# Second token pair's first block sums during h times M, casts by kind, and products that wait for their own part of a weight pair

## The chip, the cores and the metric

The kernel runs on one core of a Trainium2 chip. The metric is the device time of one launch in microseconds, the median of three runs.

## The reference

An attention with mixing of heads before and after the softmax, then two chained feed-forward layers, all in float32:

```python
scores = scale * np.matmul(q, k.transpose(0, 1, 3, 2))          # 4 x 12 heads, 448 x 64
scores = np.einsum('bhij,hg->bgij', scores, w_pre)
attn = softmax(scores)                                          # over the last axis
attn = np.einsum('bhij,hg->bgij', attn, w_post)
x = np.matmul(attn, v)                                          # -> 1792 tokens x 768
h = (x @ w1) * (x @ w2)                                         # 1792 x 1024
x = (h @ w3) @ w_out                                            # 1792 x 768
h = x @ w_in                                                    # 1792 x 2048
out = np.square(np.maximum(h, 0)) @ w_out2                      # 1792 x 768
```

## The kernel before

Every float32 operand of a product is split into two float16 halves, high and low, and a product is three matmuls (high x high, high x low, low x high). A cast of an operand is thus two instructions: ScalarE writes the high half (`nc.scalar.activation` with AF.Copy), VectorE the low half (`scalar_tensor_tensor`, the scaled operand minus its high half).

The stages, with their place in the profiled execution: attention to about 425 us; the two hidden products and their product h to 655; M = w3 x w_out, which takes the place of two products, to 725 (`m_tile`, matmuls L1520); h x M to 836 (matmuls L1243, evicted by ScalarE L1710); x times w_in to 1036 (`multiply_in`, L1847); and the last product with w_out to the end (`multiply`, L2099).

The last two stages use a seven-product scheme for 2 x 2 blocks. Of a weight pair q = 0..7 there are the blocks A11, A12, A22 and the sums S1 to S4; of a token pair t = 0, 1 the blocks B11, B21, B22 and the sums T1 to T4. S3 = a11 - a21, S1 = a21 + a22, S2 = S1 - a11, S4 = a12 - S2; T1 = b12 - b11, T3 = b22 - b12, T2 = b22 - T1, T4 = b21 - T2. GpSimd makes the sums, ScalarE and VectorE the casts. Each of the seven products of (q, t) is 9 matmuls of 448 columns. TensorE takes them in the order A11 of the n-th pair, S1 of the one before, S3, A12, S2, S4 of the one before, A22; the pairs (q, t) come as (0,0), (1,0), (2,0), (1,1), (2,1), (0,1), (3,0) and so on.

The work beside the products is written as Python generators (streams), each a chain of steps with an engine and a planned cost. `tick(us)` is called behind products in the code and advances the planned time by that much; the planner then takes steps whose engine is free by plan. What it takes is put into the engine's queue there, and each engine runs its queue in that order. `finish(stream)` takes all that is left of a stream at once.

The streams that matter here are:

- `form_in` (L1061): per weight pair q it loads two blocks (tiles ib), makes the four sums on GpSimd (L1073) and casts them on ScalarE (L1124) and VectorE (L1125), into tile w for q = 0 and wq from q = 1. For q below 3 the sums lie in two tiles it: ta with sums[0] = S1 and sums[1] = S2, tb with S3 and S4, where the positions in wq are A11, A12, A22, then ta, then tb. A product asks `need_in(q)`, which takes steps until all of the pair is cast.
- `x2_steps` (L1654): for a token pair, per block column c of three, the casts B (ScalarE L1434, VectorE L1430) and the sums T on GpSimd (L1658). It begins for t = 1 when the last eviction of h x M is issued. B11 of t = 1 is cast before, in a stream `first_of`.
- `keep_m` (L1499): in the M stage, copies of the two product banks by ScalarE, and as a stream the reductions of their largest values on VectorE (L1261). In the same stage VectorE decodes weights that come in packed, with three instructions each (L776, L779, L783), then ScalarE and GpSimd split them (L991, L994) into the operand w of the M products. `m_tile` ticks 0.163 per product bank after each of the three matmuls of a bank.
- `mixed_tokens` (L1966): in the w_out stage, for each of 14 token tiles, four sums on GpSimd (L1969) and seven casts on ScalarE (L1991) and VectorE (L1992). The products' evictions are ScalarE's L2113 and VectorE's L2115; those of the w_in stage are ScalarE's L1882 and L1892 and VectorE's L1884.

Of the kernel before, what the change touches and what calls it, by code (L numbers as in the profile page):

```python
# [34 lines left out]
def talking_heads_attention_moe_moe2(  # L35
# [1025 lines left out]
    def form_in():  # L1061

        for g in range(NF2 // IG):
            box = {}

            def sides(q):
                box["b"] = [flat(w_tile(1, "ib")) for _ in range(2)]
                flush("kept")
                for z in range(2):
                    nc.sync.dma_start(box["b"][z], kept_in[2 * q + z])  # L1070

            def mix(o, a, b, op=ALU.subtract):
                nc.gpsimd.tensor_tensor(o, a, b, op=op)  # L1073

            for q in range(g * IG // 2, (g + 1) * IG // 2):
                while ("in", 2 * q + 1) not in wsp:
# [4 lines left out]
                if q < 3:
                    ta, tb = (flat(w_tile(1, "it")) for _ in range(2))
                    sums = [ta[:, :OH], ta[:, OH:], tb[:, :OH], tb[:, OH:]]
                else:
                    while x_of[1] in streams:
                        yield REST, 0.5, lambda: finish(x_of[1])
                    sums = [stage()[:, :OH] for _ in range(4)]
                a11, a12, a21, a22 = x0[:, :OH], x0[:, OH:], x1[:, :OH], x1[:, OH:]
                for o, l, r, op in (
                    (sums[0], a21, a22, ALU.add), (sums[1], sums[0], a11, ALU.subtract),  # L1090
                    (sums[2], a11, a21, ALU.subtract), (sums[3], a12, sums[1], ALU.subtract),
                ):
# [4 lines left out]
                if q:
                    while not started or (q > 2 and q - 2 not in over):
                        yield REST, 0.5, lambda: None
                    w = fin_pool[0].tile([P, 2, 7, OH], F16, tag="wq", name="wq", bufs=2)  # L1100
                    ks = [w[:, :, k] for k in range(7)]

                    def where(k, n):
                        return [w[:, z, k : k + n].rearrange("p k o -> p (k o)") for z in range(2)]

                else:
                    ws = [w_tile(0).rearrange("p z (k o) -> p z k o", k=2) for _ in range(4)]
                    ks = [ws[k][:, :, z] for k, z in ((0, 0), (0, 1), (1, 0), (2, 0), (2, 1), (3, 0), (3, 1))]

                    def where(k, n):  # L1110
                        i, y = ((0, 0), (0, 1), (1, 0), (2, 0), (2, 1), (3, 0), (3, 1))[k]
                        return [ws[i][:, z, y : y + n].rearrange("p k o -> p (k o)") for z in range(2)]

                srcs = [(x0, 0, 2), (x1[:, OH:], 2, 1)]
                if q < 3:
                    srcs += [(ta, 3, 2), (tb, 5, 2)]
# [2 lines left out]
                parts = [(x, k, where(k, n)) for x, k, n in srcs]
                for x, k, (h, l) in parts:  # L1120
                    n = x.shape[-1] // OH
                    if k == 3:
# [524 lines left out]
    def xop(t, z, k, c):  # L1647
# [3 lines left out]
            return xs_[z][:, 7, c]  # L1651
        return xbig[0][:, z, k - 1, c]

    def x2_steps(t, ts):  # L1654
        box = {}

        def mix(o, a, b):
            nc.gpsimd.tensor_tensor(o, a, b, op=ALU.subtract)  # L1658

        def mixes(c):  # L1660
            b11, b12, b21, b22 = ts[c], ts[NDC + c], ts[c + 3], ts[NDC + c + 3]
            box[c] = {B11: b11, B21: b21, B22: b22, T1: b11, T2: b22, T3: b12, T4: b21}
            t1, t2, t3, t4 = (box[c][k] for k in (T1, T2, T3, T4))
            return [
                (POOL, 1.25, lambda: mix(t1, b12, b11)), (POOL, 1.25, lambda: mix(t3, b22, b12)),
                (POOL, 1.25, lambda: mix(t2, b22, t1)), (POOL, 1.25, lambda: mix(t4, b21, t2)),
            ]
# [8 lines left out]
        sums = [mixes(c) for c in range(3)]  # L1676
        for c in range(3):
            yield from casts(c, (B21, B22) if t else (B11, B21, B22))
            if t == 0:
                yield from sums[c]  # L1680
                yield after(POOL)
                yield from casts(c, (T3, T2, T4, T1))
            elif c:
                yield from sums[c - 1]
        if t:
            yield from sums[2]
            for k in (T3, T2, T4, T1):
                for c in range(3):
                    yield from casts(c, (k,))

    have_x, first_of = [set(), set()], []

    def casts_of(t, c, ks):
        yield from halves_steps(
            [([xop(t, z, k, c) for z in range(2)], x, x_scale[0][0]) for k, x in ks]
        )
        for k, _ in ks:
            have_x[t].add((k, c))
# [594 lines left out]
```

## Time and profile before

| | us |
|---|---|
| median of 3 runs | 1234.51 (1233.56 to 1236.69) |
| the profiled execution | 1236.24 |
| its span, first to last instruction | 1234.5 |
| TensorE busy | 1213.4 |
| VectorE busy | 948.6 |
| ScalarE busy | 804.5 |
| GpSimd busy | 581.6 |

The profile is that of one execution; its time lies a little above the median. TensorE is PE in the profile's rows, its weight loads PEld, VectorE is DVE, ScalarE ACT, GpSimd POOL. A row "x<-a,b" writes x from a and b. A releaser, as in "[3.17 <-DVE wq L1125]", is the instruction that ended an engine's idle time of that length.

### The profile page before, as it was taken

What the parts mean: (1) busy time and instruction counts of PE and PEld (TensorE: products, weight loads), DVE (VectorE), ACT (ScalarE), POOL (GpSimd) and SP (SyncE); (2) the same over time, 40 slices, a digit from 0 to 9 for tenths busy, and PEclk for the clock granted to TensorE, in tenths of its full rate; (3) what the DMA queues carried; (4) which work ended last, traced back from release to release, by engine and by line L of the source; (5) the groups of instructions that cost most, each with busy time, mean ns of one, the idle gap of its engine ahead of it and who ended that gap; (6) DMA issues with size and microseconds to landing.
All of it is one profiled execution on the core that took longest, in us unless ns stands there. A gap on an engine that the chain in (4) does not pass through costs nothing.

```text
span 1234.5 us, 26238 instructions
## 1 busy us (share of the span) xinstructions
PE 1213.4 (98%) x9904; PEld 749.2 (61%) x9904; DVE 948.6 (77%) x1690; ACT 804.5 (65%) x1620; POOL 581.6 (47%) x569
## 2 busy tenths in 40 slices
PE   7999999999999999999999999998999999999998
PEld 3666776677667655555558975554455555666665
DVE  6888899788889957766665875787578774999783
ACT  6788888888888735655554454567778785765430
POOL 3898788889878600110011211526124423667340
PEclk9999999999999999999999999999999999999999
DMA  6456555655645934755524547263478659565562
GB/s 186 123 156 166 141 146 134 169 128 155 171 114 164 260 98 120 159 143 163 133 94 145 171 146 243 76 207 103 143 269 289 237 169 320 180 189 181 171 201 77
DMA packets 139843, 205.02 MB, mean 166 GB/s; under 512 B 33764, under 2 KB 114788, under 8 KB 139716
## 3 DMA queue, kind: packets, MB, share of 16 engines
q1 hardware_dynamic: 136020, 200.01, 54.7%
q10 hardware_dynamic: 3136, 2.40, 0.8%
q8 instruction: 78, 1.28, 0.5%
q0 software_dynamic: 560, 0.93, 0.4%
q14 instruction: 49, 0.40, 0.1%
HBM read 114.60 MB, written 50.16 MB: 133 GB/s over the span
## 4 chain that ended last, share of the span: by engine, by line
PE 80%; DVE 9%; DMA 5%; ACT 2%; issue 1%; POOL 1%; SPq 0%; ACTq 0%; DVEq 0%; POOLq 0%
PE mm L1243 20%; PE mm L2099 15%; PE mm L1847 13%; PE p L284 10%; PE o L380 9%; PE s L241 5%; PE a L494 5%; DVE x L1430 2%; DMA Bt<-S 2%; PE p L1243 2%; DVE xa L776 1%; DVE xa L779 1%; DVE xa L783 1%; DMA raw<-in_moe_w_dram 1%; DVE wq L1125 1%
## 5 line engine op out<-in xcount | busy, mean ns | idle before, releaser
L1243 PE MATMUL mm<-x,w 128*128 128x448 f16 x1044 | 197.7, 352 | 0.0
L1847 PE MATMUL mm<-x,wq 128*128 128x448 f16 x882 | 172.7, 356 | 5.3 <-DVE wq L1125 3.7
L1243 PEld LDWEIGHTS <-w 128*128 128x128 f16 x1152 | 112.2, 98 | 104.3
L284 PE MATMUL p<-Bt,wpre_k 120*120 120x448 f32 x360 | 159.5, 561 | 4.9 <-DMA Bt<-S 4.2
L2099 PEld LDWEIGHTS <-ao 128*128 128x128 f16 x1176 | 115.0, 98 | 77.1 <-issue 1.2
L380 PEld LDWEIGHTS <-EH 120*112 120x112 f16 (+1 forms) x1440 | 124.9, 130 | 44.6 <-issue 37.1
L1847 PEld LDWEIGHTS <-wq 128*128 128x128 f16 x882 | 86.4, 99 | 87.4 <-DVE wq L1125 4.5
L353 POOL TENSOR_SCALAR EH<-E,st 120x448 f16<-120x448 f32 (+1 forms) x152 | 113.1, 752 | 49.1 <-DVE st L336 37.0
L402 DVE TENSOR_TENSOR ATl<-o,ATh 112x480 f16<-112x480 f32 x180 | 116.0, 645 | 22.3 <-ACT ATh L396 21.6
L306 ACT ACTIVATE E<-p,st 120x448 f32<-120x448 f32 x180 | 116.0, 645 | 22.9 <-DVE st L298 14.2
L396 ACT CAST ATh<-o 112x480 f16<-112x480 f32 x180 | 101.2, 562 | 44.3 <-PE o L380 39.4
L380 PE MATMUL o<-wph,EH 120*112 120x120 f16 x720 | 124.6, 219 | 1.0 <-DVE ATl L402 1.0
L380 PE MATMUL o<-wph,EL 120*112 120x120 f16 x720 | 122.6, 216 | 0.0
L380 PE MATMUL o<-wpl,EH 120*112 120x120 f16 x720 | 122.6, 216 | 0.0
L365 POOL TENSOR_TENSOR EL<-F,EH 120x448 f16<-120x448 f32 (+1 forms) x90 | 104.1, 1157 | 32.8 <-issue 19.9
L298 DVE TENSOR_REDUCE st<-p 120x1 f32<-120x448 f32 x180 | 110.1, 612 | 3.1 <-PE p L284 2.8
L1243 PE MATMUL mm<-h,M 128*128 128x448 f16 x576 | 110.2, 353 | 0.0
L2099 PE MATMUL mm<-x,ao 128*128 128x384 f16 x588 | 96.6, 326 | 1.0 <-ACT st L2113 1.0
L2099 PE MATMUL mm<-ow,ao 128*128 128x384 f16 x588 | 96.0, 326 | 0.0
L380 PEld LDWEIGHTS <-EL 120*112 120x112 f16 x720 | 93.9, 130 | 0.0
L367 DVE SCALAR_TENSOR_TENSOR EL<-E,st,EH 120x448 f16<-120x448 f32 (+1 forms) x90 | 83.6, 929 | 10.9 <-POOL EH L353 10.5
L1243 PEld LDWEIGHTS <-M 128*128 128x128 f16 x576 | 55.9, 98 | 52.0 <-DVE M L1430 0.8
(264 smaller groups left out, 2532.9 us busy)
## 6 DMA issues: line engine op xcount, KB each, us to landing
Bt<-S SPq DMA_DIRECT2D x176, 210.0 KB
raw<-in_moe_w_out_dram SPq DMA_DIRECT2D x24, 768.0 KB
g<-ev SPq DMA_DIRECT2D x64, 224.0 KB
gt<-g SPq DMA_DIRECT2D x56, 256.0 KB
raw<-in_moe_w_in_dram SPq DMA_DIRECT2D x16, 768.0 KB
raw<-in_moe_w_dram SPq DMA_DIRECT2D x14, 768.0 KB
raw<-in_moe_w_dram SPq DMA_DIRECT2D x16, 512.0 KB
kept_out<-xa SPq DMA_DIRECT2D x16, 384.0 KB
```

Source lines behind the costliest of these rows:

```text
L284: nc.tensor.matmul(pt[: n * H, :S], wpre_k.rearrange("p t g -> p (t g)")[: n * H, : n * H], Bt.pop(u)[: n * H], start=True, stop=True,)
L298: nc.vector.tensor_reduce(nsum[u][:n, 0, j : j + 1], Pp[u][:n, :S], axis=AX.X, op=ALU.max, negate=True)
L306: nc.scalar.activation(e[:n], Pp.pop(u)[:n, :S].rearrange("p (a b) -> p a b", a=EG), AF.Exp, bias=t[:n, 0, j : j + 1], scale=1.0, accum_ou ...
L353: nc.gpsimd.tensor_scalar(seven(EH[u][:n]), Ex[u][:n], inverse(u), 1.0, op0=ALU.mult, op1=ALU.mult)
L365: nc.gpsimd.tensor_tensor(a, f, b, op=ALU.subtract)
L367: nc.vector.scalar_tensor_tensor(a, e, inverse(u), b, op0=ALU.mult, op1=ALU.subtract)
L380: nc.tensor.matmul(pt[:CP, c * n : (c + 1) * n], a[:n, c * CP : (c + 1) * CP], w[:n, :n], start=(i == 0), stop=(i == 2),)
L396: nc.scalar.copy(ATs[s][0][:, :, :, m * NR : m * NR + nr], src)
L402: nc.vector.tensor_tensor(ATs[s][1][:, :, :, a], src, ATs[s][0][:, :, :, a], op=ALU.subtract)
L1243: nc.tensor.matmul(pt[:, :S], w[a][:, cs], x[z][:, sl], start=(c == 0 and i == 0), stop=(c == len(parts) - 1 and i == 2),)
L1847: nc.tensor.matmul(pt[:, :S], w[:, a, c * P : (c + 1) * P], xop(t, b, kb, c), start=(start and c == 0 and m == 0), stop=(c == 2 and m == 2 ...
L2099: nc.tensor.matmul(pt[:, :OH], y[:, a, q * P : (q + 1) * P], ow[g, q][kb][:, w], start=(start and q == 0 and m == 0), stop=(q == NQ - 1 an ...
```

## The change

The set of instructions is the same on each engine, and the products stand in the same order on TensorE. What differs is the order in the other queues.

In the M stage `m_tile` ticks only where it works on one bank. Where it works on two, the caller ticks once, 0.98, behind all six matmuls:

```diff
-            tick(0.163 * len(os_))
+            if len(os_) == 1:
+                tick(0.163)
...
             m_tile(ws, c, acc, c == 0, c == NFC - 1, os_)
+            if len(os_) == 2:
+                tick(0.98)
```

In VectorE's queue of that stage, around the decode of a 768 wide weight that ends at 680.91 us in the trace, before:

```order
L776 TENSOR_SCALAR xa<-raw 128x768
L779 SCALAR_TENSOR_TENSOR xa<-raw,xa 128x768
L783 SCALAR_TENSOR_TENSOR xa<-zt,xa 128x768
L776 TENSOR_SCALAR xa<-raw 128x512
L779 SCALAR_TENSOR_TENSOR xa<-raw,xa 128x512
L783 SCALAR_TENSOR_TENSOR xa<-zt,xa 128x512
L776 TENSOR_SCALAR xa<-raw 128x512
L779 SCALAR_TENSOR_TENSOR xa<-raw,xa 128x512
L783 SCALAR_TENSOR_TENSOR xa<-zt,xa 128x512
L1261 TENSOR_REDUCE mx<-st 128x1 x2
L776 TENSOR_SCALAR xa<-raw 128x512
```

and now (L1266 is the former L1261):

```order
L776 TENSOR_SCALAR xa<-raw 128x768
L779 SCALAR_TENSOR_TENSOR xa<-raw,xa 128x768
L783 SCALAR_TENSOR_TENSOR xa<-zt,xa 128x768
L1266 TENSOR_REDUCE mx<-st 128x1 x2
L776 TENSOR_SCALAR xa<-raw 128x512
L779 SCALAR_TENSOR_TENSOR xa<-raw,xa 128x512
L783 SCALAR_TENSOR_TENSOR xa<-zt,xa 128x512
L1266 TENSOR_REDUCE mx<-st 128x1 x2
L776 TENSOR_SCALAR xa<-raw 128x512
L779 SCALAR_TENSOR_TENSOR xa<-raw,xa 128x512
L783 SCALAR_TENSOR_TENSOR xa<-zt,xa 128x512
```

The first two pairs of reductions stood three and four decodes behind the wide one; now they stand right behind it and one decode later.

In `form_in` the parts of a weight pair are grouped and cast in the order in which products use them, and a product waits for its own part:

```diff
-                    sums = [ta[:, :OH], ta[:, OH:], tb[:, :OH], tb[:, OH:]]
+                    s3, s2, s1, s4 = ta[:, :OH], ta[:, OH:], tb[:, :OH], tb[:, OH:]
...
-                srcs = [(x0, 0, 2), (x1[:, OH:], 2, 1)]
+                in_w[q] = (ks, lo)
+                srcs = [(x0, A11, 2)]
                 if q < 3:
-                    srcs += [(ta, 3, 2), (tb, 5, 2)]
+                    srcs += [(ta, S3, 2), (a22, A22, 1), (tb, S1, 2)]
                 else:
-                    srcs += [(x, 3 + k, 1) for k, x in enumerate(sums)]
+                    srcs += [(s3, S3, 1), (s2, S2, 1), (a22, A22, 1), (s1, S1, 1), (s4, S4, 1)]
...
+                    have_w.update((q, PLACE.index(PLACE[k] + i)) for i in range(n))
...
-    def need_in(q):
+    def need_in(q, k):
...
-        while q not in in_w:
-            assert forming[0].step(True) or q in in_w
-        return in_w[q]
+        while (q, k) not in have_w:
+            assert forming[0].step(True) or (q, k) in have_w
+        return in_w[q][0][k]
```

For t = 1 the sums T1 and T3 become streams of their own during h x M, one behind each eviction of its last token block (i == 3), and the casts come by kind instead of by block column:

```diff
+    def lower(o, a, b):
+        nc.gpsimd.tensor_tensor(o, a, b, op=ALU.subtract)
...
         if t:
-            finish(first_of[0])
+            for st in sums_of:
+                finish(st)
             while not fin_pool:
                 yield REST, 0.5, lambda: None
+            yield from cast(B22, b22)
+            for c in range(3):
+                yield POOL, 1.25, lambda: lower(b22[c], b22[c], b11[c])
+            yield from cast(T3, b12)
+            yield from cast(B21, b21)
+            for c in range(3):
+                yield POOL, 1.25, lambda: lower(b21[c], b21[c], b22[c])
+            for k, xs in ((T2, b22), (T4, b21), (T1, b11)):
+                yield from cast(k, xs)
+            return
...
+    def first_sum(ts, c):
+        if c < 3:
+            finish(first_of[0])
+            o, a, b = ts[c], ts[NDC + c], ts[c]
+        else:
+            o, a, b = ts[NDC + c - 3], ts[NDC + c], ts[NDC + c - 3]
+        yield POOL, 1.25, lambda: lower(o, a, b)
...
+            if i == 3:
+                sums_of.append(Stream(first_sum(ts, c)))
+                streams.append(sums_of[-1])
```

GpSimd's queue from the sums of q = 0 (the first four rows) to those of q = 2, before:

```order
L1073 TENSOR_TENSOR it<-ib 128x384
L1073 TENSOR_TENSOR it<-it,ib 128x384
L1073 TENSOR_TENSOR it<-ib 128x384
L1073 TENSOR_TENSOR it<-ib,it 128x384
L1658 TENSOR_TENSOR st<-st 128x448 x4
L1073 TENSOR_TENSOR it<-ib 128x384
L1073 TENSOR_TENSOR it<-it,ib 128x384
L1073 TENSOR_TENSOR it<-ib 128x384
L1073 TENSOR_TENSOR it<-ib,it 128x384
L1658 TENSOR_TENSOR st<-st 128x448 x20
L1073 TENSOR_TENSOR it<-ib 128x384
L1073 TENSOR_TENSOR it<-it,ib 128x384
L1073 TENSOR_TENSOR it<-ib 128x384
L1073 TENSOR_TENSOR it<-ib,it 128x384
```

and now (L1077 was L1073, L1663 was L1658):

```order
L1077 TENSOR_TENSOR it<-ib 128x384 x2
L1077 TENSOR_TENSOR it<-it,ib 128x384
L1077 TENSOR_TENSOR it<-ib,it 128x384
L1663 TENSOR_TENSOR st<-st 128x448 x4
L1077 TENSOR_TENSOR it<-ib 128x384 x2
L1077 TENSOR_TENSOR it<-it,ib 128x384
L1077 TENSOR_TENSOR it<-ib,it 128x384
L1663 TENSOR_TENSOR st<-st 128x448 x17
L1077 TENSOR_TENSOR it<-ib 128x384 x2
L1077 TENSOR_TENSOR it<-it,ib 128x384
L1077 TENSOR_TENSOR it<-ib,it 128x384
L1663 TENSOR_TENSOR st<-st 128x448 x3
```

Of the 24 block sums 20 stood in one piece ahead of the sums of q = 2; now 17 stand there, six of them queued during h x M, and the three T4 sums come behind.

VectorE's queue where the w_in products begin (x_12921 and x_12927 are the casts of the second token pair, wq those of the pair q = 1), before, down to the cast of tb with S3:

```order
L1745 TENSOR_REDUCE om<-osum 128x1
L1125 SCALAR_TENSOR_TENSOR wq<-ib,is,wq 128x384
L1884 SCALAR_TENSOR_TENSOR ev<-mm,sci,ev 128x448
L1430 SCALAR_TENSOR_TENSOR x_12921<-st,xs,x_12921 128x448 x2
L108 TENSOR_SCALAR is<-mm 128x1
L109 TENSOR_SCALAR is<-is 128x1
L112 TENSOR_SCALAR is<-is 128x1
L113 RECIPROCAL is<-is 128x1
L1055 TENSOR_TENSOR sci<-xs,is 128x1
L1125 SCALAR_TENSOR_TENSOR wq<-it,is,wq 128x768
L1884 SCALAR_TENSOR_TENSOR ev<-mm,sci,ev 128x448
L1125 SCALAR_TENSOR_TENSOR wq<-it,is,wq 128x768
```

and now, from the B22 casts to the second tile it:

```order
L1435 SCALAR_TENSOR_TENSOR x_12927<-st,xs,x_12927 128x448 x3
L1130 SCALAR_TENSOR_TENSOR wq<-ib,is,wq 128x768
L1760 TENSOR_REDUCE om<-osum 128x1
L1435 SCALAR_TENSOR_TENSOR x_12927<-st,xs,x_12927 128x448
L1130 SCALAR_TENSOR_TENSOR wq<-it,is,wq 128x768
L1898 SCALAR_TENSOR_TENSOR ev<-mm,sci,ev 128x448
L1130 SCALAR_TENSOR_TENSOR wq<-ib,is,wq 128x384
L1130 SCALAR_TENSOR_TENSOR wq<-it,is,wq 128x768
L1435 SCALAR_TENSOR_TENSOR x_12927<-st,xs,x_12927 128x448
```

The tile with S3 (the first wq<-it) stands behind one other wq cast now, and only behind B22 and one T3 cast.

In `mixed_tokens` the sums keep their order and the casts change theirs:

```diff
             yield POOL, 1.35, lambda: add(s3, a11, a21, ALU.subtract)
+            yield from part(A11, a11)
             yield POOL, 1.35, lambda: add(s1, a21, a22, ALU.add)
-            yield from part(A11, a11)
+            yield from part(A12, a12)
+            yield from part(S3, s3)
             yield POOL, 1.35, lambda: add(s2, s1, a11, ALU.subtract)
-            yield from part(S3, s3)
-            yield from part(A12, a12)
+            yield from part(A22, a22)
             yield POOL, 1.35, lambda: add(a12, a12, s2, ALU.subtract)
+            yield from part(S1, s1)
             yield from part(S2, s2)
-            yield from part(A22, a22)
-            yield from part(S1, s1)
             yield after(POOL)
             yield from part(S4, a12)
```

ScalarE's queue at the second token tile, where the w_out products begin (ao<-gt is a cast of a plain block or of S4, ao<-ss of a sum, L2113 a product's eviction), before, from 1038.51 us in the trace on:

```order
L1991 ACTIVATE ao<-gt,gs 128x512
L2113 ACTIVATE st<-mm,sv 128x384
L1991 ACTIVATE ao<-ss,gs 128x512
L1991 ACTIVATE ao<-gt,gs 128x512
L1991 ACTIVATE ao<-ss,gs 128x512
L1991 ACTIVATE ao<-gt,gs 128x512
L2113 ACTIVATE st<-mm,sv 128x384
L1991 ACTIVATE ao<-ss,gs 128x512
L1892 ACTIVATE ev<-mm,sci 128x448
```

and now (L2005 was L1991, L2127 was L2113):

```order
L2005 ACTIVATE ao<-gt,gs 128x512 x2
L2005 ACTIVATE ao<-ss,gs 128x512
L2127 ACTIVATE st<-mm,sv 128x384
L2005 ACTIVATE ao<-gt,gs 128x512
L2005 ACTIVATE ao<-ss,gs 128x512
L2127 ACTIVATE st<-mm,sv 128x384
L2005 ACTIVATE ao<-ss,gs 128x512
L1906 ACTIVATE ev<-mm,sci 128x448
```

Behind A11 stood an eviction, then S3, A12, S2 and A22 in one piece ahead of the next eviction. Now A11, A12 and S3 stand ahead of the first eviction, only A22 and S1 ahead of the next, and S2 behind that one.

## Rows read from the trace of the kernel before

**Rows 1.** The page's busy time, us (share of span) xinstructions of each engine
```profile
PE 1213.4 (98%) x9904; PEld 749.2 (61%) x9904; DVE 948.6 (77%) x1690; ACT 804.5 (65%) x1620; POOL 581.6 (47%) x569
```

**Rows 2.** Waits of TensorE: us in total, times, longest us; the stages touched
```profile
PE mm L1847 <- DVE wq L1125: 3.7, 2, 3.2
PE mm L1847 <- ACT wq L1124: 1.6, 1, 1.6
...
PE mm L2099 <- ACT st L2113: 1.0, 1, 1.0
...
PE mm L1520 <- ACT w L991: 0.7, 1, 0.7
PE mm L1520 <- POOL w L994: 0.6, 2, 0.4
```

**Rows 3.** Windows: length, busy PE PEld DVE ACT POOL, granted clock, DMA share, GB/s
```profile
852.27:855.43 3.16, 3.16 (x10) 1.29 (x11) 0.73 (x2) 0.37 (x2) 3.01 (x3) 0.53 0.20 73
...
863.71:869.05 5.34, 4.83 (x16) 2.04 (x17) 4.08 (x9) 3.87 (x7) 0.00 (x0) 0.68 0.58 175
869.05:880.39 11.34, 11.34 (x61) 5.88 (x60) 3.82 (x10) 7.08 (x15) 3.91 (x4) 1.00 0.34 128
...
1050.00:1075.00 25.00, 25.00 (x155) 15.03 (x154) 24.79 (x34) 16.50 (x27) 13.96 (x11) 1.00 0.69 212
```

**Rows 4.** Timeline 838 to 870, the stall of q = 1: start, us, engine, operation
```profile
837.98 3.35 DVE L1430 SCALAR_TENSOR_TENSOR x<-st,xs,x 128x448 f16<-128x448 f32 x4 [1.97 <-ACT x L1434]
...
839.40 15.01 POOL L1658 TENSOR_TENSOR st<-st 128x448 f32<-128x448 f32 x10 [1.78 <-DVE x L1430]
...
845.07 2.44 DVE L1430 SCALAR_TENSOR_TENSOR x<-st,xs,x 128x448 f16<-128x448 f32 x2
...
846.36 1.75 ACT L1124 ACTIVATE wq<-it,is 128x768 f16<-128x768 f32 x2
...
848.45 1.97 DVE L1125 SCALAR_TENSOR_TENSOR wq<-it,is,wq 128x768 f16<-128x768 f32 x1
...
850.33 0.67 DVE L1884 SCALAR_TENSOR_TENSOR ev<-mm,sci,ev 128x448 f32<-128x448 f32 x1
850.93 1.29 DVE L1125 SCALAR_TENSOR_TENSOR wq<-it,is,wq 128x768 f16<-128x768 f32 x1
...
852.27 6.34 PE L1847 MATMUL mm<-x,wq 128*128 128x448 f16 x25 [3.17 <-DVE wq L1125]
```

**Rows 5.** The same timeline, the casts and products of q = 2
```profile
856.33 3.38 DVE L1430 SCALAR_TENSOR_TENSOR x<-st,xs,x 128x448 f16<-128x448 f32 x3 [3.33 <-ACT x L1434]
...
860.22 1.27 DVE L1430 SCALAR_TENSOR_TENSOR x<-st,xs,x 128x448 f16<-128x448 f32 x2
...
863.69 1.55 DVE L1125 SCALAR_TENSOR_TENSOR wq<-ib,is,wq 128x768 f16<-128x768 f32 x2 [0.77 <-ACT wq L1124]
...
863.71 0.55 PE L1847 MATMUL mm<-x,wq 128*128 128x448 f16 x2 [1.58 <-ACT wq L1124]
...
864.77 2.15 PE L1847 MATMUL mm<-x,wq 128*128 128x448 f16 x7 [0.50 <-DVE wq L1125]
```

**Rows 6.** Timeline of GpSimd, 806 to 838, its last sum in h x M
```profile
836.48 1.14 POOL L1658 TENSOR_TENSOR st<-st 128x448 f32<-128x448 f32 x1 [13.25 <-ACT st L1710]
```

**Rows 7.** Timeline of VectorE from 679, and of all engines from 698, M stage
```profile
682.61 0.69 DVE L783 SCALAR_TENSOR_TENSOR xa<-zt,xa 128x512 int32<-128x512 int32 x1 [0.64 <-ACT zt L775]
684.19 1.47 DVE L776 TENSOR_SCALAR xa<-raw 128x512 int32<-128x512 int32 x1 [0.89 <-DMA raw<-in_moe_w_dram]
...
687.10 1.00 DVE L1261 TENSOR_REDUCE mx<-st 128x1 f32<-128x384 f32 x2
...
706.56 0.98 PE L1520 MATMUL mm<-wo,w 128*128 128x384 f32 x4 [0.75 <-ACT w L991]
```

**Rows 8.** Timeline 1036 to 1052, the first products of w_out
```profile
1043.55 1.60 POOL L1969 TENSOR_TENSOR ss<-ss,gt 128x512 f32<-128x512 f32 x1
...
1046.42 0.56 ACT L2113 ACTIVATE st<-mm,sv 128x384 f32<-128x384 f32 x1
...
1047.03 5.20 PE L2099 MATMUL mm<-x,ao 128*128 128x384 f16 x31 [0.96 <-ACT st L2113]
```

More of the change, by code (lines that the diff above doesn't have):

```diff
@@ L999, in talking_heads_attention_moe_moe2 @@
     in_w, x_of, over = {}, [], set()
+    A11, A12, A22, S1, S2, S3, S4 = range(7)
     fin_pool = []
@@ L1059, in have_scale @@
         finish(scaling[g])
+    have_w = set()
+    PLACE = (0, 1, 2, 5, 4, 3, 6)
     def form_in():
@@ L1086, in form_in @@
                         yield REST, 0.5, lambda: finish(x_of[1])
-                    sums = [stage()[:, :OH] for _ in range(4)]
+                    s3, s2, s1, s4 = (stage()[:, :OH] for _ in range(4))
                 a11, a12, a21, a22 = x0[:, :OH], x0[:, OH:], x1[:, :OH], x1[:, OH:]
                 for o, l, r, op in (
-                    (sums[0], a21, a22, ALU.add), (sums[1], sums[0], a11, ALU.subtract),
-                    (sums[2], a11, a21, ALU.subtract), (sums[3], a12, sums[1], ALU.subtract),
+                    (s3, a11, a21, ALU.subtract), (s1, a21, a22, ALU.add),
+                    (s2, s1, a11, ALU.subtract), (s4, a12, s2, ALU.subtract),
                 ):
@@ L1100, in form_in @@
                     w = fin_pool[0].tile([P, 2, 7, OH], F16, tag="wq", name="wq", bufs=2)
-                    ks = [w[:, :, k] for k in range(7)]
+                    ks = [w[:, :, k] for k in PLACE]
                     def where(k, n):
@@ L1107, in form_in @@
                     ws = [w_tile(0).rearrange("p z (k o) -> p z k o", k=2) for _ in range(4)]
-                    ks = [ws[k][:, :, z] for k, z in ((0, 0), (0, 1), (1, 0), (2, 0), (2, 1), (3, 0), (3, 1))]
+                    at_ = ((0, 0), (0, 1), (1, 0), (2, 0), (2, 1), (3, 0), (3, 1))
+                    ks = [ws[at_[k][0]][:, :, at_[k][1]] for k in PLACE]
                     def where(k, n):
-                        i, y = ((0, 0), (0, 1), (1, 0), (2, 0), (2, 1), (3, 0), (3, 1))[k]
+                        i, y = at_[k]
                         return [ws[i][:, z, y : y + n].rearrange("p k o -> p (k o)") for z in range(2)]
-                srcs = [(x0, 0, 2), (x1[:, OH:], 2, 1)]
+                in_w[q] = (ks, lo)
+                srcs = [(x0, A11, 2)]
                 if q < 3:
-                    srcs += [(ta, 3, 2), (tb, 5, 2)]
+                    srcs += [(ta, S3, 2), (a22, A22, 1), (tb, S1, 2)]
                 else:
-                    srcs += [(x, 3 + k, 1) for k, x in enumerate(sums)]
[L1119 to L1122, printed above, removed]
+                    srcs += [(s3, S3, 1), (s2, S2, 1), (a22, A22, 1), (s1, S1, 1), (s4, S4, 1)]
+                for x, k, n in srcs:
+                    h, l = where(PLACE[k], n)
+                    if k == S3:
                         yield after(POOL)
@@ L1652, in xop @@
         return xbig[0][:, z, k - 1, c]
+    def lower(o, a, b):
+        nc.gpsimd.tensor_tensor(o, a, b, op=ALU.subtract)
     def x2_steps(t, ts):
[L1655 to L1667, printed above, removed]
@@ L1669, in casts, with cast @@
-        def casts(c, ks):
-            yield from casts_of(t, c, [(k, box[c][k]) for k in ks])
+        b11, b21, b12, b22 = (ts[i : i + 3] for i in range(0, 2 * NDC, 3))
+        def cast(k, xs, cs=range(3)):
+            return casts_of(t, cs, k, [xs[c] for c in cs])
         if t:
-            finish(first_of[0])
+            for st in sums_of:
+                finish(st)
             while not fin_pool:
                 yield REST, 0.5, lambda: None
-        sums = [mixes(c) for c in range(3)]
@@ L1677, in x2_steps @@
-        for c in range(3):
[L1678 to L1698, printed above, removed]
+            yield from cast(B22, b22)
[5 more added lines that the diff above has]
+                yield POOL, 1.25, lambda: lower(b21[c], b21[c], b22[c])
@@ new lines, in x2_steps @@
+            for k, xs in ((T2, b22), (T4, b21), (T1, b11)):
+                yield from cast(k, xs)
+            return
+        for c in range(3):
+            for k, xs in ((B11, b11), (B21, b21), (B22, b22)):
+                yield from cast(k, xs, (c,))
+            for o, a, b in ((b11, b12, b11), (b12, b22, b12), (b22, b22, b11), (b21, b21, b22)):
+                yield POOL, 1.25, lambda: lower(o[c], a[c], b[c])
+            yield after(POOL)
+            for k, xs in ((T3, b12), (T2, b22), (T4, b21), (T1, b11)):
+                yield from cast(k, xs, (c,))
@@ new lines, in talking_heads_attention_moe_moe2, with casts_of @@
+    have_x, first_of, sums_of = [set(), set()], [], []
+    def casts_of(t, cs, k, xs):
+        yield from halves_steps([
+            ([xop(t, z, k, c) for z in range(2)], x, x_scale[0][0]) for c, x in zip(cs, xs)
+        ])
+        have_x[t].update((k, c) for c in cs)
+    def first_sum(ts, c):
[5 more added lines that the diff above has]
+        yield POOL, 1.25, lambda: lower(o, a, b)
@@ L1714, in talking_heads_attention_moe_moe2 @@
         if i == 2:
-            first_of.append(Stream(chain(*(casts_of(1, c, [(B11, ts[c])]) for c in range(3)))))
+            first_of.append(Stream(casts_of(1, range(3), B11, ts[:3])))
             streams.append(first_of[0])
@@ L1721, in talking_heads_attention_moe_moe2 @@
     finish(x_of[0])
-    need_in(0)
+    for k in range(7):
+        need_in(0, k)
     mid.close()
@@ L1834, in talking_heads_attention_moe_moe2 @@
     xt, zt_, st_, s4_ = {}, {}, {}, {}
-    A11, A12, A22, S1, S2, S3, S4 = range(7)
     def event():
@@ L1841, in multiply_in @@
         q, t = SEQ[n]
-        w = need_in(q)[0][ka]
+        w = need_in(q, ka)
         while any((kb, c) not in have_x[t] for c in range(3)):
```

1 line of the change is left out of this document (removed).

## The prediction

> **What bounds the kernel now.** I read the page's busy table first. TensorE is busy 98% of the span [rows 1], so an edit can only win time where TensorE stands still or runs at its lower clock. Next I read TensorE's waits. Of the rows for the stages that this diff touches, the w_in products (L1847) lose 3.7 us to VectorE's casts of wq (two waits, the longest 3.2) and 1.6 us to one ScalarE cast; the w_out products (L2099) lose 1.0 us once; the M products (L1520) lose 0.7 us once and 0.6 us in two waits [rows 2]. Together 7.6 us. Then the windows of the clock: two stretches just behind the w_in waits run at a mean granted clock of 0.53 and 0.68, while the stretch after them has 1.00 [rows 3]. Full speed is 2.4 GHz, the lower level 1.2. At 0.53 over 3.16 us the clock costs 0.47 x 3.16 = 1.49 us; at 0.68 over 5.34 us it costs 0.32 x 5.34 = 1.71 us. Last I read the timeline around each wait, for what the releasing instruction had ahead of it in its own queue.
>
> The w_in loss as a whole: 3.17 us [rows 4], 1.58 and 0.50 us [rows 5], and 1.49 + 1.71 us of low clock [rows 3], in sum 8.45 us. That is where the money is. The M stage adds 1.33 us and w_out 0.96 us.
>
> **Part 1, q = 1: the stall at 849.10.** TensorE waits from 849.10 to 852.27 for the VectorE cast L1125 that begins at 850.93 [rows 4]. It makes the low halves of S3 and S4, the last tile of its weight pair. Ahead of it since 837.98 stood four B casts, two casts of ib, an eviction, two more B casts, five small scale steps (0.94 us, from 847.51 to 848.45), the 1.97 us cast of the tile with S1 and S2, and an eviction of 0.67. Beside all that GpSimd ran ten block sums in 15.01 us [rows 4]. Two prices follow for one cast. Alone, a block cast (128x448) takes 1.27 / 2 = 0.64 us, and the 1.55 us of a 768 and a 384 wide cast make 1.03 for the wide one (an estimate by width). Beside sums, three block casts took 3.38, of which the first began before the contended part, so 1.4 each [rows 5], and a wide cast 1.97 [rows 4].
>
> In the changed order S3 shares a tile with S2 and is VectorE's second wq cast. Ahead of it from 837.98 are three B22 casts (1.9 to 4.2 us), the A11/A12 cast (1.0 to 2.0), one T3 cast (0.6 to 1.4) and a short reduction; then its own 1.0 to 2.0. It ends at 842.5 at the low prices and at 847.6 at the high ones. TensorE wants it at 849.10, so even the dear end leaves 1.5 us: the 3.17 us go, and the 1.49 us of low clock with them. GpSimd's six first sums, which stood in that stretch, now follow the evictions of the h times M products; GpSimd idled 13.25 us there ahead of one sum of 1.14 us [rows 6]. They wait for ScalarE's evictions and the B11 casts, and nothing stands behind them on GpSimd until the B22 casts are done. What they can slow is weight decoding on VectorE, which no product wants soon; I cost that at nothing, and if that cover is gone it is at most 6 x (1.4 - 0.64) = 4.6 us of VectorE time.
>
> **What is late next.** After S3's cast VectorE has an eviction (0.67), A22 (0.5 to 1.0), S1/S4 (1.0 to 2.0), a T3 cast (0.6 to 1.4) and the eviction that frees the bank of A12 for q = 1. That ends between 846.0 and 853.3. TensorE, no longer stopped, wants the bank some seven matmuls after 849.10; at 11.34 / 61 = 0.19 us each [rows 3] that is about 850.4. So a wait between 0 and 2.9 us. The three T2 sums should be over at about 844 (three of 1.1 to 1.7 us behind the first B22 cast) and the next GpSimd sums wait for the A22 and S1/S4 casts, so the middle of this chain runs alone; a mixed sum gives 850.5 to 851. I take **0.6**.
>
> Then comes A11 of q = 2. Behind that eviction stand a T3 cast, the scale steps (0.94), an eviction, three B21 casts, another eviction and the wide cast: 0.6 + 0.9 + 0.7 + 1.9 + 0.7 + 1.0 = 5.8 at the low prices, 1.4 + 0.9 + 0.7 + 4.2 + 0.7 + 2.0 = 9.9 at the high ones, plus some 0.5 of reductions. TensorE comes to the low halves at about 862.13 - 3.17 - 1.49 + 0.4 = 857.9, or 858.5 with the 0.6. The cast ends between 852.3 and 863.7, mixed at 859.6 to 860.2: a wait of 0 to 5.2, I take **1.4**. Before, the same place cost 1.58 + 0.50 [rows 5]; the wait on ScalarE is the part that goes, since the casts there no longer stand behind a late eviction chain. For the clock: 1.58 + 0.50 was followed by the stretch at 0.68 (1.71 us), the 0.96 us wait of w_out and the 0.7 of M by none [rows 2, 3]; 1.4 lies between, so I take half, **0.8**, of 0 to 1.7. The w_in gain is 8.45 - 0.6 - 1.4 - 0.8 = **5.65 us**.
>
> **Part 2, M.** At 706.56 TensorE has waited 0.75 us for a cast of w3, whose decode stood on VectorE behind pairs of L1261 reductions of 1.00 us [rows 7]. The new tick puts the first pairs earlier, into VectorE's idle time: 0.64 us before 682.61 and 0.89 us before 684.19 [rows 7], so the decodes behind start up to 1.5 us sooner. The waits are 0.75, 0.4 and 0.2 us, all shorter. I take the whole **1.33 us** (0 at worst, if each pair merely swaps places with a decode that is wanted as early).
>
> **Part 3, w_out.** At 1047.03 TensorE has waited 0.96 us for the eviction L2113 that began at 1046.42, which stood in ScalarE's queue behind the casts of S2 and A22, and S2's sum ran on GpSimd from 1043.55 for 1.60 us [rows 8]. In the new order only A22 and S1 stand between that eviction and the one before it, and S2 comes behind it. I take **0.96**; if the S3 cast, third now, meets its own late sum, half a us is lost instead: -0.5 to 0.96.
>
> **Casts of later pairs** (q from 3 on, later token tiles) only change order inside a pair. TensorE shows no further wait for them in the table of waits [rows 2], and 25.00 of 25.00 us busy from 1050 to 1075 [rows 3]; nothing is costed.
>
> **Sum.** 5.65 + 1.33 + 0.96 = 7.9 us. The profiled execution took 1236.24 us, 1.7 more than its span of 1234.5; so 1228.3 on its scale. It lies 1.73 above the median of the runs, 1234.51, so the median should be **1226.6 us**.
>
> **A rule against the change.** Rows first: ten sums took 15.01 us, 1.5 each, against 1.14 for one with VectorE quiet, and block casts beside them 1.4 against 0.64 [rows 4 to 6]. If the two engines simply took turns, ten sums (11.4) and the casts that lay in that stretch (three block casts 1.9, three wide 3.1, one half-wide 0.5) would need 16.9 us, not 15.01. So they slow each other, but by less than taking turns. The Trainium skill, page SBUF — State Buffer, section Who interferes with whom, says that a VectorE instruction with two SBUF inputs and a GpSimd instruction that reads SBUF exclude each other, the second blocking until the first ends; by that, the trace agrees in kind and falls short in size, and the first rival below is what the rule would make of it.
>
> **Rivals.** (a) Taking turns: from 837.98 to A11 of q = 2 lie nine block casts (5.8), four wide and one half-wide cast (4.6) and ten sums (11.4), 21.8 us, plus 1.4 of scale steps and reductions: 861.2, a wait of 2.7 instead of 1.4, with the whole 1.7 of low clock. The w_in gain is then 8.45 - 0.6 - 2.7 - 1.7 = 3.45, the total 5.7, the median 1228.8. For it: each contended price above. Against: the 15.01. (b) Nothing is left over: 8.45 + 2.29 = 10.7, median 1223.8. For it: the low prices leave slack at each place. (c) The change doesn't do what it says: S3's cast is second in VectorE's queue, but its high half on ScalarE, behind evictions that wait for TensorE, is late, and the stall stays for the most part. With a w_in gain of 1 the total is 3.3, median 1231.2, no difference. Against: in the trace ScalarE's high halves run well ahead of VectorE's [rows 4]. (d) Slower: in the w_out stage each of 14 token tiles gets a cast on ScalarE that waits for a sum (S3, third now) with a product's eviction right behind it. If TensorE lost one sum, 1.60 us, per tile, that is 22.4 - 7.9 = 14.5 us more, 1249. It is slower from (7.9 + 3.7) / 14 = 0.83 us per tile. Against: one such wait of 0.96 in the whole stage now [rows 2], none once the casts have run ahead [rows 3].
>
> **How the numbers follow.** A measurement of this kernel tells 0.3%, 3.7 us, from no change: faster is below 1230.8, slower above 1238.2. The forecast has 0.55, (a) 0.16, (b) 0.10, (c) 0.13, (d) 0.06. Faster is forecast, (a) and (b): 0.81; same 0.13; slower 0.06. The range runs from 1223.0, just under (b), to 1231.0, over (a) and the forecast with waits of twice my values and into (c); what it leaves out is (d) and about half of (c), with a little on the low side.
>
> **What would show it.** Right: no TensorE wait of over 1 us between 845 and 853, S3's low half cast before 848, GpSimd's first sums of the second pair between 820 and 840; a wait under 2 us near 858; no wait at the first w_out products and at most 0.3 us in M. Wrong: a stretch at a clock near 0.5 behind 849 again; a wait of over 2.5 us at A11 of q = 2; waits of w_out products that repeat per tile.

## The result and the profile after

The changed kernel takes 1222.48 us (median of 5 runs, 1222.17 to 1223.14) against 1234.42 us before (5 runs, 1232.27 to 1236.69): a ratio of 0.9905, 95% interval 0.9891 to 0.992, 11.9 us less. Forecast were 1226.6 us and 7.9 us less, range 1223.0 to 1231.0. The direction was right, the size was not, and the time lies 0.5 us below the range.

The page after, TensorE's share, and all that is left of TensorE's waits over 0.5 us (us in total, times, longest):

```profile
PE 1206.9 (99%) x9904; PEld 746.7 (61%) x9904; DVE 948.8 (78%) x1690; ACT 804.5 (66%) x1620; POOL 587.6 (48%) x569
```

```profile
PE p L284 <- DMA Bt<-S: 3.1, 5, 1.1
PE p L284 <- ACT ATh L396: 1.4, 2, 1.2
PE a L635 <- DVE ATl L630: 1.3, 1, 1.3
PE o L380 <- DVE ATl L402: 1.1, 3, 0.5
PE p L284 <- ACT w L890: 0.9, 1, 0.9
PE p L1248 <- DMA x<-x_d: 0.7, 1, 0.7
PE s L241 <- DVE kl L192: 0.6, 1, 0.6
```

All belong to the attention and the first products. Against [rows 2], no product of M, w_in or w_out (now L1525, L1861, L2113) waits at all. The clock is whole as well; the windows around the old stalls (length, busy PE, PEld, DVE, ACT, POOL, granted clock, DMA share, GB/s), against 0.53 and 0.68 in [rows 3]:

```profile
825.00:850.00 25.00, 25.00 (x135) 12.96 (x134) 20.05 (x31) 18.97 (x36) 14.07 (x10) 1.00 0.53 181
850.00:875.00 25.00, 25.00 (x133) 12.92 (x132) 18.36 (x32) 21.99 (x47) 11.49 (x9) 1.00 0.34 115
```

Where the time came from is read most safely from stage lengths, since two executions also differ in the attention. The groups by line give the first and last start of each product group (us), for before

```profile
L1520 PE MATMUL mm<-wo,w x192: 333/334/497, 655.3 to 722.5; 128*128 128x384 f32 x192
L1520 PE MATMUL mm<-late,w x192: 333/334/446, 672.1 to 725.1; 128*128 128x384 f32 x192
...
L1847 PE MATMUL mm<-x,w x126: 351/352/353, 836.1 to 924.5; 128*128 128x448 f16 x126
...
L2099 PE MATMUL mm<-x,ao x588: 323/326/337, 1036.4 to 1142.9; 128*128 128x384 f16 x196
L2099 PE MATMUL mm<-ow,ao x588: 326/326/326, 1131.4 to 1230.7; 128*128 128x384 f16 x196
```

and after

```profile
L1525 PE MATMUL mm<-wo,w x192: 333/334/497, 653.9 to 718.7; 128*128 128x384 f32 x192
L1525 PE MATMUL mm<-late,w x192: 333/334/444, 670.7 to 721.3; 128*128 128x384 f32 x192
...
L1861 PE MATMUL mm<-x,w x126: 352/352/363, 832.3 to 911.9; 128*128 128x448 f16 x126
...
L2113 PE MATMUL mm<-x,ao x588: 326/326/337, 1023.8 to 1129.2; 128*128 128x384 f16 x196
L2113 PE MATMUL mm<-ow,ao x588: 326/326/326, 1117.7 to 1217.0; 128*128 128x384 f16 x196
```

| stage (first start to first start of the next, or last start) | before | after | less | forecast |
|---|---|---|---|---|
| M: 655.3 to 725.1, 653.9 to 721.3 | 69.8 | 67.4 | 2.4 | 1.33 |
| w_in: 836.1 to 1036.4, 832.3 to 1023.8 | 200.3 | 191.5 | 8.8 | 5.65 |
| w_out: 1036.4 to 1230.7, 1023.8 to 1217.0 | 194.3 | 193.2 | 1.1 | 0.96 |

The three make 12.3 us, close to the 11.9 between the medians. M starts 1.4 us earlier in the execution after, ahead of anything that the change touches; that is scatter between executions (over the first 40 us TensorE's mean granted clock was 0.91 in the one before and 1.00 in the one after).

### The profile page after: what moved, and what is told of

The parts are those of the page before. It is cut to its first block, busy times and chain, and to the rows that moved or that the text cites. A ratio compares the mean times of both kernels' runs of the same rounds, so it can differ in the third digit from the quotient of the medians.

```text
span 1220.8 us, 26222 instructions
## 1 busy us (share of the span) xinstructions
PE 1206.9 (99%) x9904; PEld 746.7 (61%) x9904; DVE 948.8 (78%) x1690; ACT 804.5 (66%) x1620; POOL 587.6 (48%) x569
## 4 chain that ended last, share of the span: by engine, by line
PE 90%; DMA 4%; DVE 3%; ACT 1%; issue 0%; SPq 0%; ACTq 0%; POOL 0%
PE mm L1248 25%; PE mm L2113 16%; PE mm L1861 16%; PE p L284 9%; PE o L380 7%; PE mm L1525 5%; PE s L241 5%; PE a L494 4%; DMA Bt<-S 2%; PE p L1248 2%; DVE ATl L402 1%; DMA x<-x_d 1%; DVE EL L367 1%; DVE st L298 1%; ACT E L306 0%; DMA vraw<-in_v_dram 0%
## 5 line engine op out<-in xcount | busy, mean ns | idle before, releaser
L1861 PE MATMUL mm<-x,wq 128*128 128x448 f16 x882 | 169.2, 352 | 0.0
L2113 PEld LDWEIGHTS <-ao 128*128 128x128 f16 x1176 | 115.0, 98 | 76.0
L1861 PEld LDWEIGHTS <-wq 128*128 128x128 f16 x882 | 86.0, 98 | 79.6
L2113 PE MATMUL mm<-x,ao 128*128 128x384 f16 x588 | 96.5, 326 | 0.0
L2113 PE MATMUL mm<-ow,ao 128*128 128x384 f16 x588 | 96.0, 326 | 0.0
```

Source lines behind the costliest of these rows:

```text
L1861: nc.tensor.matmul(pt[:, :S], w[:, a, c * P : (c + 1) * P], xop(t, b, kb, c), start=(start and c == 0 and m == 0), stop=(c == 2 and m == 2 ...
L2113: nc.tensor.matmul(pt[:, :OH], y[:, a, q * P : (q + 1) * P], ow[g, q][kb][:, w], start=(start and q == 0 and m == 0), stop=(q == NQ - 1 an ...
```

## The experiments

In the first four, one part of the change is undone. Their ratios to before have intervals some 0.4% wide, more than some parts are worth, and before itself took 1232.06 us beside e1 to e4 and 1232.36 beside e5 to e7, against 1234.42 beside the change. So the stage lengths of their traces, taken as above, carry the verdicts, and each trace is of one execution. Where two kernels have the same matmuls in the same order, the start of each is also compared with that of the same matmul in the other trace.

**e1: the old ticks in M.**

```diff
-            if len(os_) == 1:
-                tick(0.163)
+            tick(0.163 * len(os_))
...
-            if len(os_) == 2:
-                tick(0.98)
```

> The changed kernel with the old three ticks in the M stage, all else as changed. Theory (queue order in M): the three waits of M products near 706, 708 and 718 us of the old clock come back, and each costs its listed wait plus the weight load that it leaves uncovered, together 2.4 us as the traces of before and after lie apart there: about 1224.9 us. Rival (the M stage gave only the listed 1.33 us and the rest is scatter between two executions): about 1223.8 us.

Measured: 1224.12 us (ratio to before 0.9939, 0.9918 to 0.9959). The M stage takes 69.5 us (652.8 to 722.3) instead of 67.4. Two of the three waits are back, 0.73 and 0.65 us, together 1.4, but the stage is 2.1 us longer. Timeline of e1 (start, us, engine, operation):

```profile
703.99 0.65 PEld L1525 LDWEIGHTS mm<-wo,w 128*128 128x128 f32 x4 [1.05 <-ACT w L991]
...
703.99 0.98 PE L1525 MATMUL mm<-wo,w 128*128 128x384 f32 x4 [0.73 <-ACT w L991]
...
705.62 3.44 PEld L1525 LDWEIGHTS mm<-wo,w 128*128 128x128 f32 x20 [0.98 <-POOL w L994]
705.62 3.76 PE L1525 MATMUL mm<-wo,w 128*128 128x384 f32 x20 [0.65 <-POOL w L994]
```

The late operand here is the stationary one, so the weight load waits too, 1.05 and 0.98 us. Start by start, TensorE falls 1.0 us behind the kernel after at the first of these places and 0.8 at the second, together 1.8 of the stage's 2.1. The matmul rows show less, 1.4, because a row counts its last matmul as busy for 0.33 us, while in a stream the next one starts 0.18 behind it (20 matmuls in 3.76 us). The median lies nearer to the rival's 1223.8 than to 1224.9; it is the stage length, 2.1 and not 1.33, that speaks for the theory, with two waits and not three.

**e2: the old order of casts in w_out.** The diff is that of the change for `mixed_tokens`, reversed.

> The changed kernel with the old order of casts in the w_out stage. Theory: one wait of about 1 us on ScalarE's eviction comes back at the second token tile and nowhere else, 1.1 us: about 1223.6 us. Rival (the w_in stage ends earlier relative to loads, so that place has slack by itself): no wait, 1222.5 us.

Measured: 1222.84 us (0.993, 0.9909 to 0.9951). The one wait on ScalarE's eviction (L2127) is back, 0.8 us; w_out takes 194.2 us (1022.4 to 1216.6) instead of 193.2. No other w_out product waits. The place and the size are the theory's; the median alone can't tell it from the rival's 1222.5.

**e3: weight pairs as before, sums and casts of the second token pair new.**

```diff
-                    s3, s2, s1, s4 = ta[:, :OH], ta[:, OH:], tb[:, :OH], tb[:, OH:]
+                    sums = [ta[:, :OH], ta[:, OH:], tb[:, :OH], tb[:, OH:]]
...
-        w = need_in(q, ka)
+        w = need_in(q)[0][ka]
```

> The changed kernel with weight pairs as before: S1 with S2 and S3 with S4, S3 cast last, products wait for the whole pair; GpSimd's first sums early and casts by kind as changed. Theory A (what stood beside VectorE's casts set their length, so early sums carry the gain): the S3 cast ends about 845.5 to 847 against a need at 845.2, a wait of 0 to 1.5 us: 1222.5 to 1225 us. Theory B (S3's place in the queue carries the gain): the stall of 3 us comes back with the low clock, 1227 to 1230 us.

**e4: the second token pair as before, weight pairs new.**

```diff
-            if i == 3:
-                sums_of.append(Stream(first_sum(ts, c)))
-                streams.append(sums_of[-1])
...
-            yield from cast(B22, b22)
+            yield from casts(c, (B21, B22) if t else (B11, B21, B22))
```

> The changed kernel with the second token pair's sums and casts as before (none during h times M, casts by block column); weight pairs in the new order with waits for the own part. Theory A (early sums carry the gain): the stall moves to another product of q = 1 or q = 2, 1227 to 1230 us. Theory B (S3's place carries it): S3's cast ends near 845.3 against 849.1 on the old clock and the casts of q = 2 stand ahead of T casts, so little is lost: 1222.5 to 1224.5 us.

Measured: e3 1222.75 us (0.9924, 0.9907 to 0.9941), e4 1224.68 us (0.994, 0.9923 to 0.9956). The w_in stage takes 192.1 us in e3 (831.6 to 1023.7) and 194.4 us in e4 (831.4 to 1025.8), against 191.5 with both parts and 200.3 with neither. TensorE's waits in the touched stages, all of e3 and then all of e4:

```profile
PE mm L1859 <- DVE wq L1129: 0.4, 1, 0.4
```

```profile
PE mm L1858 <- DVE ev L1895: 2.1, 4, 1.2
```

So each part alone takes away most of the 8.8: 8.2 us the early sums with casts by kind, 5.9 us the new weight pairs. Theory B falls with e3 (S3's place was undone and no stall came back), and theory A with e4 (the sums were late, and no stall of its size came at a product of q = 1 or 2; the median lies 0.2 us above theory B's range). The early sums and the casts by kind were not tried apart, so e3 doesn't tell which of them does it. In e4 the second wq cast, S3's, begins at 838.71 and takes 1.81 us beside sums, well ahead of its product; what is left are four waits on VectorE's evictions L1895, 0.23 us at 849.34 and the others from 910 us on, the longest 1.24 us at 947.98.

**e5: both w_in parts undone, M and w_out changed.** The diff is that of the change, w_in parts reversed.

> The kernel before with only the M tick and the order of casts in w_out changed; both w_in parts as before. Theory (the two w_in parts are each nearly enough alone, but one of them is needed): the stall of 3 us for S3's cast, the low clock and the waits at q = 2 come back, together 8.8 us against the changed kernel: about 1231.3 us. Rival (the w_in stage behaves otherwise once the M stage ends earlier): under 1228 us.

Measured: 1230.09 us (0.9976, 0.9964 to 0.9987). The w_in stage takes 199.6 us (830.8 to 1030.4), 8.1 us more than after: the waits are back at S3 (3.55 us) and q = 2 (1.86 and 0.50). The two parts are stand-ins for one another, so that undoing them singly, as e3 and e4 do, sums to 3.5 us and not to 8.1.

**e6: before, without the second token pair's sums.** What is left out is GpSimd's work alone; VectorE's order is that of before.

```diff
         def mix(o, a, b):
-            nc.gpsimd.tensor_tensor(o, a, b, op=ALU.subtract)
+            if t == 0:
+                nc.gpsimd.tensor_tensor(o, a, b, op=ALU.subtract)
```

> The kernel before with the second token pair's twelve block sums on GpSimd left out (its T operands then hold unsummed blocks), all queues else in the same order. Theory A (S3's cast was late because sums beside VectorE's casts made them about twice as long): at the alone prices S3's cast ends near 846 on the old clock against a need at 849.1, the stall and its low clock are gone, and the sums of q = 2 are early, so the w_in loss of 8.8 us goes: about 1223.5 to 1226 us. Theory B (its place as last cast made it late, whatever GpSimd does): a stall of 2 us or more stays at the third matmul of S3 and the time is above 1229 us.

Measured: 1228.4 us (0.9972, 0.9961 to 0.9982); w_in takes 194.1 us (833.5 to 1027.6), 6.2 us less than before. Timeline, the last two wq casts of q = 1, S3's third matmul, and the products of q = 2 with ScalarE's eviction (L1893) and cast ahead of them:

```profile
843.64 1.02 DVE L1125 SCALAR_TENSOR_TENSOR wq<-it,is,wq 128x768 f16<-128x768 f32 x1 [1.05 <-ACT wq L1124]
...
845.17 1.38 DVE L1125 SCALAR_TENSOR_TENSOR wq<-it,is,wq 128x768 f16<-128x768 f32 x1
...
846.60 4.91 PE L1848 MATMUL mm<-x,wq 128*128 128x448 f16 x25 [0.18 <-DVE wq L1125]
...
854.32 0.62 ACT L1893 ACTIVATE ev<-mm,sci 128x448 f32<-128x448 f32 x1
...
855.55 1.43 ACT L1124 ACTIVATE wq<-ib,is 128x768 f16<-128x768 f32 x2
...
856.52 0.55 PE L1848 MATMUL mm<-x,wq 128*128 128x448 f16 x2 [1.50 <-ACT wq L1124]
...
857.58 1.50 PE L1848 MATMUL mm<-x,wq 128*128 128x448 f16 x7 [0.50 <-DVE wq L1125]
```

S3's cast is still the last, yet its product waits 0.18 us instead of 3.17 [rows 4]: in this queue order, VectorE's casts beside sums made that stall, so theory A holds for q = 1 and theory B falls. The waits of q = 2 stay at 1.50 and 0.50 with GpSimd idle (from 855.02 to 856.52 it has no instruction), so sums beside casts are not their cause: their casts stand behind evictions in ScalarE's queue, which has no gap there. For q = 2 theory A was wrong, and the median is 2.4 us above its range.

**e7: the changed kernel with each T2 sum issued twice.**

```diff
-                yield POOL, 1.25, lambda: lower(b22[c], b22[c], b11[c])
+                yield POOL, 1.25, lambda: [lower(b22[c], b22[c], b11[c]) for _ in range(2)]
```

> The changed kernel with each of the three T2 sums issued twice on GpSimd (the second spoils T2, so that the output is not the reference's), VectorE's queue in the same order. Theory A (VectorE's casts stretch to 1.5 to 1.9 us whenever GpSimd has sums in hand): the casts of S3, A22 and S1/S4 take 1.0, 0.8 and 0.9 us longer, the eviction for A12 of q = 1 ends near 848.8 against a need at about 846.6, a wait of 1 to 2.5 us there and one near A11 of q = 2: 1224 to 1227 us. Theory B (VectorE keeps its alone prices when its casts follow one another without a gap, and GpSimd is the one held up): no wait of over 0.5 us, 1222.5 to 1223.2 us.

Measured: 1224.51 us (0.9926, 0.9906 to 0.9947); w_in takes 195.8 us (831.2 to 1027.0), 4.3 us more than after. Timeline:

```profile
833.32 12.11 POOL L1663 TENSOR_TENSOR st<-st 128x448 f32<-128x448 f32 x8 [2.45 <-ACT st L1721]
...
841.14 1.88 DVE L1130 SCALAR_TENSOR_TENSOR wq<-it,is,wq 128x768 f16<-128x768 f32 x1
...
844.36 1.89 DVE L1130 SCALAR_TENSOR_TENSOR wq<-it,is,wq 128x768 f16<-128x768 f32 x1
846.17 1.48 DVE L1435 SCALAR_TENSOR_TENSOR x<-st,xs,x 128x448 f16<-128x448 f32 x1
...
847.57 0.67 DVE L1898 SCALAR_TENSOR_TENSOR ev<-mm,sci,ev 128x448 f32<-128x448 f32 x1
...
848.29 4.99 PE L1861 MATMUL mm<-x,wq 128*128 128x448 f16 x18 [2.65 <-DVE ev L1898]
```

GpSimd is at sums until 845.43, and at those of q = 2 from 846.17. The casts of S3, S1/S4 and T3 take 1.88, 1.89 and 1.48 us beside them, and TensorE waits 2.65 us for the very eviction that the prediction named, followed by 3.31 us at a mean granted clock of 0.56. Theory A, but for its second wait: none comes near A11 of q = 2. The four executions took 1221.64 to 1225.65 us and the trace is of the slowest, so the loss need not be this large in each.

## Why the prediction was right and wrong

**Right: the places and their causes.** Each wait that the sum took away in M, at S3 and in w_out is gone. Two of the three in M came back with the tick (e1), the one in w_out with its casts (e2), and S3's only with both w_in parts undone (e5). Rival (c), that the stall stays, fell; rival (d) too, since no w_out product waits after.

**Wrong: the 2.8 us left over in w_in.** The steps that failed are the waits of 0.6 at A12 of q = 1 and of 1.4 at A11 of q = 2, and with them the 0.8 of low clock. All are zero: rival (b), given 0.10, is what came. The rows after (timeline, times 3.8 us earlier than in before):

```profile
834.03 7.41 POOL L1663 TENSOR_TENSOR st<-st 128x448 f32<-128x448 f32 x5 [2.45 <-ACT st L1721]
...
835.00 3.63 DVE L1435 SCALAR_TENSOR_TENSOR x<-st,xs,x 128x448 f16<-128x448 f32 x3 [1.45 <-ACT x L1439]
...
838.55 1.89 DVE L1130 SCALAR_TENSOR_TENSOR wq<-ib,is,wq 128x768 f16<-128x768 f32 x1
...
840.52 2.68 SPq L1074 DMA_DIRECT2D ib<-kept_in  x2
...
841.84 1.00 DVE L1130 SCALAR_TENSOR_TENSOR wq<-it,is,wq 128x768 f16<-128x768 f32 x1
...
844.86 5.27 PE L1861 MATMUL mm<-x,wq 128*128 128x448 f16 x27
...
845.42 0.67 DVE L1898 SCALAR_TENSOR_TENSOR ev<-mm,sci,ev 128x448 f32<-128x448 f32 x1
...
846.33 2.18 POOL L1077 TENSOR_TENSOR it<-ib 128x384 f32<-128x384 f32 x2 [4.89 <-DMA ib<-kept_in]
...
848.47 1.85 DVE L1435 SCALAR_TENSOR_TENSOR x<-st,xs,x 128x448 f16<-128x448 f32 x3
...
848.58 2.61 POOL L1077 TENSOR_TENSOR it<-it,ib 128x384 f32<-128x384 f32 x1
...
851.09 1.02 DVE L1130 SCALAR_TENSOR_TENSOR wq<-ib,is,wq 128x768 f16<-128x768 f32 x1 [0.17 <-ACT wq L1129]
...
852.08 3.01 PE L1861 MATMUL mm<-x,wq 128*128 128x448 f16 x15
```

The first half went as the forecast's dear prices had it: three B22 casts in 3.63 us, the A11/A12 cast 1.89. Then GpSimd was done with its sums at 841.44 and idle for 4.89 us. The prediction had it wait there for the A22 and S1/S4 casts; but the last of these was over at 844.89, and the row names the load of the next weight blocks (ib), issued from 840.52 on. With GpSimd still, S3's cast took 1.00, and the eviction for A12 was over at 846.09, or 849.9 on the clock of before (3.8 more): forecast were 850.5 to 851 against a need at 850.4. TensorE came to A12 at about 846.6 (844.86 and nine matmuls of S3 at 0.19, an estimate), 850.4 on the old clock. So the need was right, the chain was 0.6 to 1.1 us too dear, and some 0.5 us was to spare.

The larger miss is A11 of q = 2, where the cast ends at 852.11, 855.9 on the old clock, against a forecast of 859.6 to 860.2. From the eviction's end that is 6.0 us, against 5.8 plus 0.5 at the low prices, 9.9 plus 0.5 at the high ones and 9.1 in the forecast's mixed sum. TensorE came to it when forecast: nine matmuls of the row at 852.08 belong to A22 of q = 1, so its third matmul starts at about 854.2 (an estimate), 858.0 on the old clock, and 2 us were to spare. The three B21 casts, 1.9 to 4.2 in the forecast, took 1.85 together, although GpSimd had sums in hand: here the sum paid. It began at 848.58, behind a cast that began at 848.47, and took 2.61 us. In before, the same kind of sum took 1.00 where VectorE stood still, and the next one 1.48 behind a cast that began 0.07 ahead of it [rows 5]:

```profile
855.44 1.00 POOL L1073 TENSOR_TENSOR it<-it,ib 128x384 f32<-128x384 f32 x1
...
856.40 1.48 POOL L1073 TENSOR_TENSOR it<-ib 128x384 f32<-128x384 f32 x1
```

The forecast knew that sums slow down too (15.01 us for ten), but it let the casts of this stretch pay as well; that a run of casts can keep its price while the sum alone pays it had not considered. The last cast also took 1.02, not up to 2.0. On the Trainium skill's page SBUF — State Buffer, section Who interferes with whom, issue order decides which of the two blocks; by that, the row at 848.58 agrees, as the later one was held up. The page's lock for one whole instruction isn't what the row shows: the 1.6 us over 1.00 reach to about the end of the third cast (850.32), not of the first. Why the casts paid beside the T2 sums and the sum paid here stays open.

That nothing was left over at A12 is luck: e7 shows it. With three sums more, the wait there, which the prediction had bounded by 0 and 2.9, is 2.65 us. At A11 of q = 2 no run brought the wait back; what ended it there is read from these rows alone.

**Mis-sized: what a wait costs.** M was 1.33 by the matmul rows and is 2.4; w_in was 8.45 and is 8.8; w_out 0.96 and is 1.1. All three are short in the same direction. In before, the weight loads waited longer than the matmuls, at the three places in M (first three rows) and at S3's stall in w_in (the last):

```profile
706.56 0.65 PEld L1520 LDWEIGHTS mm<-wo,w 128*128 128x128 f32 x4 [1.07 <-ACT w L991]
707.92 3.44 PEld L1520 LDWEIGHTS mm<-wo,w 128*128 128x128 f32 x20 [0.71 <-POOL w L994]
...
718.48 1.54 PEld L1520 LDWEIGHTS mm<-late,w 128*128 128x128 f32 x9 [0.52 <-POOL w L994]
...
852.27 0.13 PEld L1847 LDWEIGHTS <-wq 128*128 128x128 f16 x2 [3.61 <-DVE wq L1125]
```

In M, 1.07 + 0.71 + 0.52 = 2.3 us of weight load waits stand against the 2.4 measured, and in e1 2.0 against 2.1. But this is no general price. In w_in the weight loads waited 3.61, 2.02 and 0.94 us, 6.6 together, where the matmul rows list 5.25; with the low clock that would be 9.8, and the stage lost 8.8. The starts show the loss directly: before falls behind after by 2.1 us at the three places in M (1.02, 0.56 and 0.51; the rest in steps of under 0.2 ahead of them), by 3.3, 1.75 and 0.7 at the three waits of w_in, and by 1.1 at the one of w_out. So each listed matmul wait is short by some 0.15 to 0.3 us. Most of that is the end of the row before it: a matmul counts as busy for 0.35 us, and the next would have started after 0.19 [rows 3].

**The two w_in parts.** The prediction laid the end of the S3 stall on both, S3's place and the sums that move away, without asking whether one would do. e3, e4 and e6 show three ways to end it, each enough: early sums with casts by kind, fewer casts ahead of S3's, or no sums beside them. The waits at q = 2 go with either part as well, down to 0.4 us (e3), but not with the sums left out (e6). That points to the order in ScalarE's and VectorE's queues; no run changes this order alone.

**The sum.** 7.9 forecast, + 2.8 not left over, + 1.1 in M, + 0.35 in w_in, + 0.15 in w_out = 12.3.

## What to carry to other kernels

Where a chain of casts runs beside another engine's work, lay out that other engine's queue on the same clock before choosing between the price alone and the price beside it: here the helper stood still for 4.89 us, for a load, just where it mattered. Read what a wait costs from the starts of the same matmul in both traces: matmul rows were short at each place, and weight load rows came close in M and too high in w_in. And where a change has two parts for one stall, ask of each whether it is enough by itself: they then guard each other, and the gain is not their sum.

## What the runs showed that was not expected

A cast and a sum that read SBUF beside one another can slow either engine: casts went from 0.64 to 1.48 and from 1.00 to 1.89 us (e7), or a sum from 1.0 to 2.61 us while three casts kept 0.62 each (after).

The clock does not follow the length of a wait alone. A wait of 3.17 us [rows 4] and one of 2.65 (e7) were each followed at once by some 3.3 us at 0.53 to 0.56, near the lower level. The wait of 3.55 us in e5 was followed by 4.90 us for 25 matmuls, 0.196 each, so at 2.4 GHz, and the clock fell only behind the later waits of 1.86 and 0.50 (0.84 from 857.68 to 860, 0.87 between 860 and 870). 1.50 and 0.50 us in e6 left it at 1.00, where 1.58 and 0.50 before were followed by 0.68. What makes the difference stays open; no run was made for it.
